# Six FFN blocks of 256 tokens behind the first, with new places for the attention stages, in a fused retention and bilinear FFN kernel

## The chip, the cores and the metric

The kernel runs on one core of a Trainium2 chip. The metric is device time in microseconds (us), the median of the runs in the fast state; lower is better. The engines are PE (matmul), PEld (its weight loads), DVE, ACT and POOL; SP issues most DMAs. PSUM is the memory in which the code places the results of its matmuls. Every execution has a state, slow when it is over 1.5% above the fastest of the same kernel.

## The reference, cut to what matters

```python
# q, k, v: (8, 8, 576, 64)   batch, heads, sequence, head dim
scores = scale * q @ k.T
ret    = scores * D            # D[i, j] = gamma_h ** (i - j) for i >= j, else 0
attn   = ret @ v               # -> x: 4608 tokens x 512
a, b   = x @ w_a, x @ w_b      # 512 -> 1536
out    = (a * b) @ w_out       # 1536 -> 512, float32
```

## The kernel before

The 4608 tokens are 36 chunks of 128. Attention of a chunk (with a running state in place of the full score matrix) writes 128 columns of `xT`; the FFN reads `xT` block by block. PE runs both from one stream (in the profile after, where an output waits for DVE until 186.61 us, the FFN group behind it starts after it, at 187.15 us): the FFN is a generator that yields after every matmul, and attention stages are dropped into it at fixed places. A place is counted in units, one unit being the work of one 512-column matmul.

```python
blocks = [512, 256, 384, 384] + [512] * ((NTOK - 1536) // 512)

def ffn_block(tok0, n, runs):
    # ... for each of 12 column tiles F of d_ff:
        pa = ps_ffn.tile(...)                    # ps_ffn: 3 PSUM buffers
        # 4 matmuls of n columns; then on ACT:
        nc.scalar.copy(ha[:, 0:n], pa[:, 0:n])
        pb = ps_ffn.tile(...)
        # 4 matmuls of n columns; then on DVE:
        nc.vector.tensor_tensor(hT[:, F, 0:n], has[F][:, 0:n], pb[:, 0:n], op=ALU.mult)
        pop()                                    # ONE deferred DVE piece (a mask or a scaling)
        yield n / 512, True                      # an edge: stages may start here
    # ... then n/128 output groups po, 12 matmuls each, two pop() in each
```

```python
def second_stage(g):            # g: a pair of chunks
    for i in g[1:]: state(i)
    for i in g: scores(i)       # PE; defers two masks per chunk: later.append(...)
def third_stage(g):
    flush()                     # issue all masks that are still deferred
    for i in g: outputs(i)      # PE reads the masked scores sT

# ... places (chunks, cast and turn, scores, outputs), in units:
placed = [((6, 7), 145, 178, 194), ((8,), 166, 197, 207), ((9, 10), 186, 224, 254)]
limit = 1e9
for i in range(NCH - 1, 10, -2):
    g = (i, i + 1) if i + 1 < NCH else (i,)
    third = min(starts[i] - 16, limit - 60)
    limit = third
    placed.append((g, third - 104, third - (30 if i == 11 else 36), third))
# ... at the end of every FFN block: flush()
```

From chunk 6 on, q and k are cast on POOL and turned by a DMA that SP issues ("turn"); SP also issues loads and stores.

Of the kernel before, what the change touches and what calls it, by code (L numbers as in the profile page):

```python
# [18 lines left out]
def kernel(  # L19
# [19 lines left out]
    nc = tc.nc  # L39
# [3 lines left out]
    DFF = moe_w_a.shape[1]  # L43
    NTOK = B * S
    NC = DM // 128
    NF = DFF // 128
# [4 lines left out]
    NCH = NTOK // 128  # L51
# [14 lines left out]
    def pool(name, bufs, space=None):  # L66
        kw = {} if space is None else {"space": space}
        return ctx.enter_context(tc.tile_pool(name=name, bufs=bufs, **kw))
# [5 lines left out]
    qkt_pool = pool("qkt", 6)  # L74
    st_pool = pool("st", 4)
    h_pool = pool("hT", 2)
    ha_pool = pool("ha", 6)
    o_pool = pool("osb", 4)
    PS = bass.MemoryType.PSUM
    ps_ffn = pool("ps_ffn", 3, PS)  # L80
# [5 lines left out]
    wa_r = moe_w_a.rearrange("(c p) f -> p c f", p=128)  # L86
    wb_r = moe_w_b.rearrange("(c p) f -> p c f", p=128)
    wo_r = moe_w_out.rearrange("(c p) m -> p c m", p=128)
    wa_sb = big.tile([128, NC, DFF], BF16)
    wb_sb = big.tile([128, NC, DFF], BF16)  # L90
# [69 lines left out]
        nc.vector.memset(t, 0.0)  # L160

    def load_w(f0, f1):
        nc.gpsimd.dma_start(wa_sb[:, :, f0:f1], wa_r[:, :, f0:f1])
        nc.gpsimd.dma_start(wb_sb[:, :, f0:f1], wb_r[:, :, f0:f1])

    def load_wo(i):
        nc.gpsimd.dma_start(wo_sb[:, 4 * i:4 * i + 4, :],
# [6 lines left out]
    def pop():  # L174
        if later:
            later.pop(0)()

    def flush():
        while later:
            later.pop(0)()  # L180

    def cast(i, on="pool"):

        qf, kf, vf = staged.pop(i)
        qkb = nat.tile([128, 2, DM], BF16, tag="qkb", name="qkb")
        vb = nat.tile([128, DM], BF16, tag="vb", name="vb")
        qb, kb = qkb[:, 0], qkb[:, 1]
        if on == "pool":
            nc.gpsimd.tensor_copy(qb, qf)  # L189
        else:  # L190
            nc.scalar.copy(qb, qf)  # L191
        if on == "dve":
            nc.vector.tensor_copy(kb, kf)
        else:
            nc.gpsimd.tensor_copy(kb, kf)  # L195
        nc.gpsimd.tensor_tensor(  # L196
            vb.rearrange("p (h d) -> p h d", h=H),
            vf.rearrange("p (h d) -> p h d", h=H),
            vs[:, i % PER, :].unsqueeze(2).to_broadcast([128, H, D]),
            op=ALU.mult)  # L200
        natural[i] = (qkb, qb, kb, vb)
# [9 lines left out]
    def transposes(i):  # L211

        natural_qk = natural[i][1:3]
        qkT = qkt_pool.tile([128, 2, HP, 128], BF16, tag="qkT", name="qkT")
        for w, copy in ((0, nc.scalar.copy), (1, nc.vector.tensor_copy)):
            tp = ps_att.tile([128, HP, 128], BF16, tag="att", name="tp")
            for p in range(HP):
                nc.tensor.transpose(tp[:, p, :],  # L218
                                    natural_qk[w][:, p * 128:(p + 1) * 128],
                                    identity)  # L220
            copy(qkT[:, w], tp)
        transposed[i] = qkT

    def state(i):
        m = i % PER
        if m == PER - 1:
            return
        qkb, qb, kb, vb = natural[i]
        r = slice(64, 128) if m == MID else slice(0, 128)
        if m == 0 or m == MID:  # L230
            kv_of[0] = ps_kv.tile([128, HP, 128], FP32, tag="kv", name="kv")
        kv = kv_of[0]
        for p in range(HP):
            sl = slice(p * 128, (p + 1) * 128)
            nc.tensor.matmul(kv[:, p, :], kb[r, sl], vb[r, sl],  # L235
                             start=(m in (0, MID) and p == 0), stop=True,
                             skip_group_check=True)
        st = states[i % len(states)]
        state_of[i + 1] = st
        nc.scalar.copy(st[0:64, :, 0:64], kv[0:64, :, 0:64])  # L240
        nc.scalar.copy(st[64:128, :, 64:128], kv[64:128, :, 64:128])

    def scores(i):
        qkT = transposed[i]
        ps = [ps_att.tile([128, HP, 128], FP32, tag="att", name=f"sc{hi}")
              for hi in (0, 1)]
        sT = st_pool.tile([128, 2, HP, 128], BF16, tag="sT", name="sT")
        scored[i] = sT
        for p in range(HP):
            for hi in (0, 1):  # L250
                r = slice(64 * hi, 64 * hi + 64)
                nc.tensor.matmul(ps[hi][:, p, :], qkT[r, 1, p, :],  # L252
                                 qkT[r, 0, p, :], start=True, stop=True,
                                 skip_group_check=True)
        keep = mask2 if i % PER == MID else mask

        def masked(hi):
            nc.vector.tensor_tensor(
                sT[:, hi], ps[hi],
                keep.unsqueeze(1).to_broadcast([128, HP, 128]),  # L260
                op=ALU.mult)

        later.append(lambda: masked(0))
        later.append(lambda: masked(1))

    def outputs(i, halves=False):
        m = i % PER
        qkb, qb, kb, vb = natural.pop(i)
        qkT = transposed.pop(i)
        sT = scored.pop(i)  # L270
        o = ps_att.tile([128, HP, 128], FP32, tag="att", name="o")
        if m > 0:
            st = state_of.pop(i)
            n = 64 if m == MID else 128
            for p in range(HP):
                for hi in (0, 1):
                    nc.tensor.matmul(o[64 * hi:64 * hi + 64, p, 0:n],  # L277
                                     st[:, p, 64 * hi:64 * hi + 64],
                                     qkT[:, 0, p, 0:n],
                                     start=(p == 0), stop=True,  # L280
                                     skip_group_check=True)
        for p in range(HP):
            for hi in (0, 1):
                e0 = p * 128 + 64 * hi
                nc.tensor.matmul(o[64 * hi:64 * hi + 64, p, :],  # L285
                                 vb[:, e0:e0 + 64], sT[:, hi, p, :],
                                 start=(m == 0 and p == 0), stop=True,
                                 skip_group_check=True)
        s0 = rows_of(i)[0][3]

        def scaled(c0, c1):
            nc.vector.tensor_tensor(  # L292
                xT[:, c0:c1, i * 128:(i + 1) * 128], o[:, c0:c1],
                qs[:, c0:c1, s0:s0 + 128], op=ALU.mult)

        if halves:
            later.append(lambda: scaled(0, HP // 2))
            later.append(lambda: scaled(HP // 2, HP))
        else:
            later.append(lambda: scaled(0, HP))  # L300


    blocks = [512, 256, 384, 384] + [512] * ((NTOK - 1536) // 512)
    WCOLS = [3, 4, 5]

    def ffn_block(tok0, n, runs):

# [60 lines left out]
    def warm(count):  # L368

        w = ps_ffn.tile([128, 4, 128], FP32, tag="ab", name="w")  # L370
        for _ in range(count):
            nc.tensor.matmul(w, identity,  # L372
                             identity.unsqueeze(1).to_broadcast([128, 4, 128]),
                             start=True, stop=True)

    W1, W2 = 128 * WCOLS[0], 128 * (WCOLS[0] + WCOLS[1])
    idle = {0: (0, 0), 1: (0, 3), 2: (2, 4), 3: (1, 4)}
    make_qs(0)
    make_qs(1)
# [4 lines left out]
    for i in range(4):  # L384
        if idle[i][0]:
            warm(idle[i][0])
        scores(i)
        flush()
        if i == 2:
            load_w(0, W1)  # L390
            load_w(W1, W2)
        if i < 3:
            cast(i + 1, "dve" if i == 2 else "act")
        state(i)
        if idle[i][1]:
            warm(idle[i][1])
        if i < 3:
            transposes(i + 1)
            outputs(i)
            flush()  # L400
    load_w(W2, DFF)
    for i in (0, 1, 2):
        load_wo(i)
    outputs(3, halves=True)
# [10 lines left out]
    starts, at = {}, 0.0  # L415
# [50 lines left out]
    for i, places in ((4, (110, 117, 121, 127)), (5, (127, 132, 136, 139))):  # L466
        todo += [(at, one_by_one, (what, i))
                 for at, what in zip(places, "CTSA")]
    placed = [((6, 7), 145, 178, 194), ((8,), 166, 197, 207),
              ((9, 10), 186, 224, 254)]  # L470
    limit = 1e9
    for i in range(NCH - 1, 10, -2):
        g = (i, i + 1) if i + 1 < NCH else (i,)
        third = min(starts[i] - 16, limit - 60)
        limit = third
        placed.append((g, third - 104, third - (30 if i == 11 else 36), third))
    for g, zeroth, second, third in placed:
        todo += [(zeroth, ahead, (g[-1],)), (second - 14, first_stage, (g,)),
                 (second, second_stage, (g,)), (third, third_stage, (g,))]
# [2 lines left out]
    at = 0.0  # L482
    tok = 0
    for tb, n in enumerate(blocks):
        runs = WCOLS if tb == 0 else [1] * NF
        for cost, edge in ffn_block(tok, n, runs):
            at += cost
            while todo and edge and at >= todo[0][0]:
                _, fn, args = todo.pop(0)
                fn(*args)  # L490
        flush()
        tok += n
# [30 lines left out]
```

## Time and profile before

| | before |
|---|---|
| time, median of 3 runs | 346.02 us (345.85 to 346.22) |
| span of the profiled execution | 877.8 us, state slow |

The page of that profile: the span, the busy time of each engine, and the DMA engines' busy tenths in 40 slices of the span.

```profile
span 877.8 us, 6134 instructions
...
PE 854.0 (97%) x2390; PEld 309.4 (35%) x2426; DVE 162.0 (18%) x272; ACT 112.6 (13%) x229; POOL 84.3 (10%) x121
...
DMA  9980049350090041025400650066002300000000
```

From its chain of waits in order of time (start, length, what):

```profile
318.47 2.35 PE pa L316 x4
320.81 2.48 PE pb L329 x4
323.30 2.35 PE pa L316 x4
```

Four 512-column matmuls take 2.35 us, 587 ns each. The profiled execution is 2.5 times as long as a timed one. (The mean clock of 1.00 given for this profile is no measurement: its trace holds no clock record.) An unchanged copy of the kernel, run later (before_again), left a profile in the fast state, and it is the one to compare with. Its page, same rows, with the granted clock in tenths:

```profile
span 344.6 us, 6170 instructions
...
PE 330.4 (96%) x2426; PEld 171.4 (50%) x2426; DVE 160.8 (47%) x272; ACT 112.3 (33%) x229; POOL 85.0 (25%) x121
...
PEclk9999999999999999999999999999999999999999
DMA  9999999999999993911994099507990950020002
```

PE is the bound (96% busy), and the DMA engines are at 9 tenths or more in each of the first 15 slices (129 us). The busy share of PE does not tell a slow execution from a fast one: it is 97% at 877.8 us and 96% at 344.6 us.

### The profile page before, as it was taken

Reading aid. Unit: us, or ns where it says so; the run is one execution under the profiler, and the core shown is the slowest. Engines: PE = TensorE matmul, PEld = TensorE weight load, DVE = VectorE, ACT = ScalarE, POOL = GpSimd, SP = SyncE. Lnnn points to the kernel's source line nnn. Section 1 sums busy time; section 2 is a strip of 40 time slices with the busy share of each in tenths; the row PEclk is TensorE's granted clock in tenths of the full one; section 3 lists DMA queues with packets and bytes.
Section 4 is the critical chain, followed back from the end, with each engine's and each line's share of the span. In section 5 each row is a group of like instructions: output and inputs, shape, how many; then the busy total and the mean of one; then the engine's idle time right before and its main releaser. Section 6 shows DMA issues by size and latency. Waiting matters only on the chain.

```text
span 877.8 us, 6134 instructions
## 1 busy us (share of the span) xinstructions
PE 854.0 (97%) x2390; PEld 309.4 (35%) x2426; DVE 162.0 (18%) x272; ACT 112.6 (13%) x229; POOL 84.3 (10%) x121
## 2 busy tenths in 40 slices
PE   6999999999999999999999999999999999999998
PEld 3322345344344333333333333432333333232223
DVE  4211122222121111211122112121121112201100
ACT  5111112011011101100111011101110011101110
POOL 6040002201011010002100210011000000000000
DMA  9980049350090041025400650066002300000000
GB/s 181 207 152 0 25 90 187 80 88 1 29 199 0 13 102 18 0 50 108 81 1 1 131 108 1 0 112 129 0 1 60 61 0 1 8 28 12 0 13 36
DMA packets 154333, 50.74 MB, mean 58 GB/s; under 512 B 144960, under 2 KB 149824, under 8 KB 154304
## 3 DMA queue, kind: packets, MB, share of 16 engines
q1 hardware_dynamic: 149552, 45.63, 26.6%
q0 software_dynamic: 4752, 4.72, 3.4%
q8 instruction: 19, 0.31, 0.2%
q14 instruction: 10, 0.08, 0.0%
HBM read 37.75 MB, written 9.44 MB: 54 GB/s over the span
## 4 chain that ended last, share of the span: by engine, by line
PE 97%; issue 2%; DMA 1%; SPq 0%; POOL 0%; DVE 0%; ACT 0%
PE pb L329 29%; PE pa L316 29%; PE po L349 28%; PE o L285 2%; PE kv L235 2%; PE o L277 2%; PE w L372 1%; PE tp L218 1%; DMA kf<-in_k_dram 1%; SPq L104 0%; POOL qkb L195 0%; PE sc_2460 L252 0%; PE sc_2449 L252 0%; PE sc_1402 L252 0%; PE sc_3677 L252 0%
## 5 line engine op out<-in xcount | busy, mean ns | idle before, releaser
L329 PE MATMUL pb<-xT,wb_sb 128*128 128x512 bf16 (+2 forms) x471 | 279.9, 775 | 2.7 <-issue 2.7
L316 PE MATMUL pa<-xT,wa_sb 128*128 128x512 bf16 (+2 forms) x472 | 277.3, 769 | 3.6 <-issue 3.1
L349 PE MATMUL po<-wo_sb,hT 128*128 128x512 bf16 (+1 forms) x425 | 253.2, 810 | 6.2 <-issue 6.2
L334 DVE TENSOR_TENSOR hT<-ha,pb 128x512 bf16<-128x512 bf16 (+2 forms) x120 | 76.2, 635 | 457.4 <-PE pb L329 443.3
L329 PEld LDWEIGHTS <-wb_sb 128*128 128x128 bf16 x480 | 82.8, 172 | 173.7 <-issue 168.0
L316 PEld LDWEIGHTS <-wa_sb 128*128 128x128 bf16 x480 | 80.7, 172 | 157.2 <-issue 151.4
L349 PEld LDWEIGHTS <-hT 128*128 128x128 bf16 x444 | 73.1, 169 | 162.1 <-issue 159.0
L322 ACT CAST ha<-pa 128x512 bf16<-128x512 f32 (+2 forms) x120 | 65.2, 544 | 447.1 <-PE pa L316 440.9
L196 POOL TENSOR_TENSOR vb<-vf,vs 128x512 bf16<-128x512 f32 x36 | 37.6, 1044 | 295.1 <-issue 144.3
L189 POOL CAST qkb<-qf 128x512 bf16<-128x512 f32 x30 | 18.3, 611 | 290.5 <-DMA qf<-in_q_dram 274.6
L360 DVE COPY osb<-po 128x512 f32<-128x512 f32 (+1 forms) x17 | 11.5, 676 | 175.5 <-PE po L349 175.5
L358 ACT COPY osb<-po 128x512 f32<-128x512 f32 (+1 forms) x20 | 11.5, 576 | 219.3 <-PE po L349 208.4
L292 DVE TENSOR_TENSOR xT<-o,qs 128x512 bf16<-128x512 f32 (+1 forms) x37 | 24.8, 674 | 46.8 <-PE o L285 46.8
L285 PE MATMUL o<-sT,vb 128*64 128x128 bf16 x288 | 30.4, 379 | 0.0
L235 PE MATMUL kv<-vb,qkb 128*128 128x128 bf16 (+1 forms) x128 | 25.4, 373 | 1.4 <-issue 0.9
L235 PEld LDWEIGHTS <-qkb 128*128 128x128 bf16 (+1 forms) x128 | 17.6, 161 | 22.2 <-issue 20.9
L285 PEld LDWEIGHTS <-vb 128*64 128x64 bf16 x288 | 22.3, 181 | 2.5 <-issue 2.5
L195 POOL CAST qkb<-kf 128x512 bf16<-128x512 f32 x32 | 19.7, 616 | 13.6 <-DMA kf<-in_k_dram 13.5
L252 PEld LDWEIGHTS <-qkT 64*128 64x128 bf16 x288 | 15.4, 135 | 12.6 <-issue 9.8
L218 PE MATMUL tp<-identity,qkb 128*128 128x128 bf16 x48 | 8.1, 362 | 6.0 <-ACT qkb L191 5.3
L372 PE MATMUL w<-identity 128*128 128x512 bf16 x14 | 9.3, 790 | 0.0
L218 PEld LDWEIGHTS <-qkb 128*128 128x128 bf16 x48 | 5.2, 140 | 11.1 <-ACT qkb L191 5.7
(195 smaller groups left out, 194.7 us busy)
## 6 DMA issues: line engine op xcount, KB each, us to landing
out_dram<-osb SPq DMA_DIRECT2D x35, 256.0 KB, 2.2
qf<-in_q_dram SPq DMA_DIRECT2D x32, 256.0 KB, 3.6
kf<-in_k_dram SPq DMA_DIRECT2D x32, 256.0 KB, 4.2
vf<-in_v_dram SPq DMA_DIRECT2D x32, 256.0 KB, 4.7
wo_sb<-in_moe_w_out_dram POOLq DMA_DIRECT2D x3, 512.0 KB, 17.8
qf<-in_q_dram SPq DMA_DIRECT2D x8, 128.0 KB, 3.6
kf<-in_k_dram SPq DMA_DIRECT2D x8, 128.0 KB, 3.5
vf<-in_v_dram SPq DMA_DIRECT2D x8, 128.0 KB, 3.5
```

The costliest lines, as they stand in the source:

```text
L189: nc.gpsimd.tensor_copy(qb, qf)
L195: nc.gpsimd.tensor_copy(kb, kf)
L196: nc.gpsimd.tensor_tensor(vb.rearrange("p (h d) -> p h d", h=H), vf.rearrange("p (h d) -> p h d", h=H), vs[:, i % PER, :].unsqueeze(2).to_ ...
L218: nc.tensor.transpose(tp[:, p, :], natural_qk[w][:, p * 128:(p + 1) * 128], identity)
L235: nc.tensor.matmul(kv[:, p, :], kb[r, sl], vb[r, sl], start=(m in (0, MID) and p == 0), stop=True, skip_group_check=True)
L285: nc.tensor.matmul(o[64 * hi:64 * hi + 64, p, :], vb[:, e0:e0 + 64], sT[:, hi, p, :], start=(m == 0 and p == 0), stop=True, skip_group_che ...
L292: nc.vector.tensor_tensor(xT[:, c0:c1, i * 128:(i + 1) * 128], o[:, c0:c1], qs[:, c0:c1, s0:s0 + 128], op=ALU.mult)
L316: nc.tensor.matmul(pa[:, 0:n], wa_sb[:, c, fs], xT[:, c, tok0:tok0 + n], start=(c == 0), stop=(c == NC - 1))
L322: nc.scalar.copy(ha[:, 0:n], pa[:, 0:n])
L329: nc.tensor.matmul(pb[:, 0:n], wb_sb[:, c, fs], xT[:, c, tok0:tok0 + n], start=(c == 0), stop=(c == NC - 1))
L334: nc.vector.tensor_tensor(hT[:, F, 0:n], has[F][:, 0:n], pb[:, 0:n], op=ALU.mult)
L349: nc.tensor.matmul(po[:, 0:width], hT[:, F, u * 128:(u + 1) * 128], wo_sb[:, F, cols], start=(F == 0), stop=(F == NF - 1))
```

## The change

Its intent: every block from the second to the seventh takes 256 tokens, so that each has exactly one pair of chunks to wait for, and all later pairs line up with even chunks. At start-up, k of chunk 3 is cast on DVE between the two masks of chunk 2, and one weight DMA is issued later.

```diff
-    blocks = [512, 256, 384, 384] + [512] * ((NTOK - 1536) // 512)
+    blocks = [512] + [256] * 6 + [512] * ((NTOK - 2048) // 512)
@@ start-up, chunk i of the first four
         scores(i)
-        flush()
-        if i == 2:
-            load_w(0, W1)
-            load_w(W1, W2)
-        if i < 3:
-            cast(i + 1, "dve" if i == 2 else "act")
+        pop()                          # first mask only
+        if i == 2:
+            list(load_w(0, W1))        # load_w is now a generator of two DMAs
+            second = load_w(W1, W2)
+            next(second)               # its other DMA after the loop
+        if i == 2:
+            cast(3, "dve")
+            flush()
+        else: ...
@@ places
-    placed = [((6, 7), 145, 178, 194), ((8,), 166, 197, 207),
-              ((9, 10), 186, 224, 254)]
+    placed = [((6, 7), 145, 176, 200), ((8, 9), 186, 238, 264),
+              ((10, 11), 222, 296, 324), ((12, 13), 280, 352, 384)]
-    for i in range(NCH - 1, 10, -2):
-        third = min(starts[i] - 16, limit - 60)
-        placed.append((g, third - 104, third - (30 if i == 11 else 36), third))
+    for i in range(NCH - 2, 13, -2):
+        third = min(starts[i] - 16, limit - 58)
+        placed.append(((i, i + 1), third - 104, third - 36, third))
```

Cut: `ha_pool` from 6 to 7 buffers, a renamed list, and the generator itself.

More of the change, by code (lines that the diff above doesn't have):

```diff
@@ L76 @@
     h_pool = pool("hT", 2)
-    ha_pool = pool("ha", 6)
+    ha_pool = pool("ha", 7)
     o_pool = pool("osb", 4)
@@ L162, in load_w @@
     def load_w(f0, f1):
-        nc.gpsimd.dma_start(wa_sb[:, :, f0:f1], wa_r[:, :, f0:f1])
-        nc.gpsimd.dma_start(wb_sb[:, :, f0:f1], wb_r[:, :, f0:f1])
+        for w_sb, w_r in ((wa_sb, wa_r), (wb_sb, wb_r)):
+            nc.gpsimd.dma_start(w_sb[:, :, f0:f1], w_r[:, :, f0:f1])
+            yield
     def load_wo(i):
@@ L300, in outputs @@
             later.append(lambda: scaled(0, HP))
-    blocks = [512, 256, 384, 384] + [512] * ((NTOK - 1536) // 512)
-    WCOLS = [3, 4, 5]
+    blocks = [512] + [256] * 6 + [512] * ((NTOK - 2048) // 512)
+    WRUNS = [3, 4, 5]
     def ffn_block(tok0, n, runs):
@@ L374, in warm @@
                              start=True, stop=True)
-    W1, W2 = 128 * WCOLS[0], 128 * (WCOLS[0] + WCOLS[1])
+    W1, W2 = 128 * WRUNS[0], 128 * (WRUNS[0] + WRUNS[1])
     idle = {0: (0, 0), 1: (0, 3), 2: (2, 4), 3: (1, 4)}
@@ L387 @@
         scores(i)
-        flush()
+        pop()
         if i == 2:
-            load_w(0, W1)
-            load_w(W1, W2)
-        if i < 3:
-            cast(i + 1, "dve" if i == 2 else "act")
+            list(load_w(0, W1))
[4 more added lines that the diff above has]
+            flush()
+        else:
+            flush()
+            if i < 3:
+                cast(i + 1, "act")
         state(i)
@@ L400 @@
             flush()
-    load_w(W2, DFF)
+    list(second)
+    list(load_w(W2, DFF))
     for i in (0, 1, 2):
@@ L468 @@
                  for at, what in zip(places, "CTSA")]
-    placed = [((6, 7), 145, 178, 194), ((8,), 166, 197, 207),
-              ((9, 10), 186, 224, 254)]
+    placed = [((6, 7), 145, 176, 200), ((8, 9), 186, 238, 264),
+              ((10, 11), 222, 296, 324), ((12, 13), 280, 352, 384)]
     limit = 1e9
-    for i in range(NCH - 1, 10, -2):
-        g = (i, i + 1) if i + 1 < NCH else (i,)
-        third = min(starts[i] - 16, limit - 60)
+    for i in range(NCH - 2, 13, -2):
+        third = min(starts[i] - 16, limit - 58)
         limit = third
-        placed.append((g, third - 104, third - (30 if i == 11 else 36), third))
+        placed.append(((i, i + 1), third - 104, third - 36, third))
     for g, zeroth, second, third in placed:
@@ L484 @@
     for tb, n in enumerate(blocks):
-        runs = WCOLS if tb == 0 else [1] * NF
+        runs = WRUNS if tb == 0 else [1] * NF
         for cost, edge in ffn_block(tok, n, runs):
```

## The prediction

> **The profile is not the timed state.** The timed runs take 346.0 us; the profiled execution spans 877.8 us and is marked slow. In the timeline four 128x512 matmuls take 2.35 us (587 ns each) and eight 128x256 ones 2.34 to 2.48 us.[...] Other engines' durations I take from the trace.
>
> **What bounds it.** PE: 97% busy, 97% of the chain of waits. The FFN is 1296 matmuls of 512 columns' worth[...]. Scores run in pairs (two start 10 ns apart in the timeline); the attention of 32 chunks behind the FFN is then 16 slots of 128 columns[...]. The first FFN matmul starts at 29.6 us in the trace[...].[...]
>
> **What the change moves.**
> 1. Start-up: k of chunk 3 is cast (0.42 us) before the second mask (0.68 us) on DVE, so its transposes can start about 0.6 us earlier. In the trace the four filler matmuls (2.6 us at 587 ns) hide this[...]. Estimate -0.4 us. The last wb piece, issued a microsecond later, has slack.
> 2. Blocks: 256, 384, 384 and two 256s of a 512 become six 256s.[...]
> 3. Evacuation:[...] DVE needs 0.42 for hT, and 1.1 when one mask (0.68) or xT scaling (0.69) is popped behind it[...]. The old 256 block carries six masks and three scalings[...]; the new six carry four and two each[...].
> 4. Feeding: the chain of cast, turn, load on POOL and SP gives a chunk every 4.6 us in the trace (loads 126.2, 130.6, 135.0, 140.0), turns land 4.0 us after issue. Before, chunks 6 to 8 are wanted inside one block of 72 units[...] and 9 to 12 soon after, within a few units of when their turns land; after, each pair has a block of its own. This should remove 1.5 to 3 us of PE waits at scores, which the slow profile cannot show.
>
> Sum about -1: **345.0 us**, range **342.0 to 347.8**. Faster by over 2%: 0.03; within 2%: 0.94; slower by over 2%: 0.03.
>
> **What would show it.** A profile in the fast state: DVE releasing PE at pa or pb in 256-token blocks (3), no wait of scores on a turn (4). If it is slow again, only times tell (undoing the blocks alone, or the cast order alone); its span should be within 1% of before, with 576 pa and pb weight loads each against 480.
>
> **What would make it wrong.** Feed stalls larger than I think (gain 3 to 5 us); DVE contention stronger than the PSUM slack (loss 2 to 4)[...].

Terms are cut from it, because they rested on matmul times that the one trace it had did not show: its budget of the whole time, which came to 340 to 349 us, the reason why point 1 should count in a fast run although fillers hide it in the trace, and the terms of points 2 and 3, +0.5 and +1.3 us. With -0.4 (point 1) and -1.5 to -3 (point 4) the sum came to "about -1", as it says.

## More of the kernel before

A stage can start only at an *edge*, which comes after each `pb` group (every 8 units in a 512-token block, every 4 in a 256-token one) and at some points of the output stage.

Who made PE wait in the fast execution (total us, times, longest; the `tp` line is start-up, where PE waits for its first data):

```profile
PE tp L218 <- ACT qkb L191: 5.7, 2, 5.3
PE sc L252 <- DMA qkT<-qkb: 2.4, 3, 1.3
...
PE o L285 <- DVE sT L258: 0.2, 1, 0.2
```

The idle time in this view is counted from a modelled end of the matmul before. What a wait costs is larger and is read from start to start: two `sc` matmuls that follow each other in 0.06 us otherwise stand 1.51 us apart at 79.7 us. Measured so, the waits between 56 and 94 us cost 0.53 + 0.35 + 1.46 + 0.90 = 3.2 us (chunks 7, 7, 10 and 12). The 0.35 us is a wait of `outputs` for a mask; the other three, 2.9 us, are waits of scores for a turned tile:

```profile
65.61 0.40 PE L252 MATMUL sc<-qkT 64*128 64x128 bf16 x8 [0.37 <-DMA qkT<-qkb]
...
81.21 0.40 PE L252 MATMUL sc<-qkT 64*128 64x128 bf16 x8 [1.30 <-DMA qkT<-qkb]
...
93.22 0.42 PE L252 MATMUL sc<-qkT 64*128 64x128 bf16 x8 [0.73 <-DMA qkT<-qkb]
```

## The result, and the profile after

| | median | range | runs |
|---|---|---|---|
| before | 345.94 us | 345.74 to 346.22 | 4 |
| after | 349.65 us | 349.40 to 351.13 | 4 |

The ratio is 1.0116 (95% interval 1.0086 to 1.0145). A ratio here is the mean time of one kernel's fast runs over that of the other's of the same rounds, so not quite the ratio of the medians. The change is 3.7 us slower: within 2%, but outside the predicted range. This profile came in the fast state. Its page, the same rows, the clock again included:

```profile
span 347.7 us, 6608 instructions
...
PE 329.7 (95%) x2584; PEld 190.4 (55%) x2618; DVE 163.2 (47%) x297; ACT 115.5 (33%) x252; POOL 84.7 (24%) x121
...
PEclk9999999999999999999999999999999999999999
DMA  9999999999899989868490299519980990020002
```

PE's waits:

```profile
PE tp L219 <- ACT qkb L192: 5.8, 2, 5.3
PE o L286 <- DVE sT L259: 2.4, 4, 0.6
PE sc L253 <- DMA qkT<-qkb: 1.7, 2, 0.9
...
PE pb L330 <- ACT ha L323: 0.5, 1, 0.5
```

The wait for turned tiles has shrunk from 2.4 us to 1.7 us, in two places:

```profile
64.32 0.40 PE L253 MATMUL sc<-qkT 64*128 64x128 bf16 x8 [0.94 <-DMA qkT<-qkb]
65.50 0.40 PE L253 MATMUL sc<-qkT 64*128 64x128 bf16 x8 [0.79 <-DMA qkT<-qkb]
```

In the list of waits a new line stands above it: `outputs` waits four times for a mask (`sT`). Where in time does the loss lie? The start of the first `ha` cast of each block marks PE's progress:

| token where the block starts | before_again | after | after minus before |
|---|---|---|---|
| 0 | 22.44 | 21.77 | -0.67 |
| 512 | 56.91 | 56.25 | -0.66 |
| 2048 | 170.47 | 169.41 | -1.06 |
| 2560 | 205.90 | 205.88 | -0.02 |
| 3072 | 240.99 | 241.78 | +0.79 |
| 3584 | 276.64 | 278.04 | +1.40 |
| 4096 | 311.05 | 314.17 | +3.12 |
| end | 344.57 | 347.69 | +3.12 |

At token 2048, where the 256-token blocks end, the kernel after is *ahead* by 1.06 us. All of the loss arises behind them, in blocks of 512 tokens that look the same in both kernels. (One chunk's attention, about 0.9 us, has moved over this border: by the places in the code the kernel before has finished 21 chunks at token 2048, the kernel after 20. So up to token 2048 the two kernels are about even, the earlier start included, and the stretch behind it loses 4.18 - 0.9 = 3.3 us. The two traced runs, 346.27 and 349.40 us, differ by 3.1 us, the medians by 3.7.)

Here is one of those blocks in the kernel after. PE first, in order of time (start, length, what, and in brackets the idle time before it and what ended it):

```profile
177.53 0.62 PE L253 MATMUL sc<-qkT 64*128 64x128 bf16 x16
...
184.13 1.03 PE L330 MATMUL pb<-xT,wb_sb 128*128 128x512 bf16 x4
185.09 0.41 PE L278 MATMUL o<-qkT,state 128*64 128x128 bf16 x8
...
185.78 0.22 PE L286 MATMUL o<-sT,vb 128*64 128x128 bf16 x1
186.61 0.38 PE L286 MATMUL o<-sT,vb 128*64 128x128 bf16 x7 [0.60 <-DVE sT L259]
```

DVE in the same stretch:

```profile
184.15 0.68 DVE L259 TENSOR_TENSOR sT<-sc,mask 128x512 bf16<-128x512 f32 x1
185.27 0.69 DVE L335 TENSOR_TENSOR hT<-ha,pb 128x512 bf16<-128x512 bf16 x1 [0.44 <-PE pb L330]
185.87 0.68 DVE L259 TENSOR_TENSOR sT<-sc,mask 128x512 bf16<-128x512 f32 x1
```

The last mask starts at 185.87 us, behind the `hT` multiply of the last `pb` group; the output matmul that reads it would have started at 185.83 and starts at 186.61, 0.77 us late before rounding. The other three blocks show the same 0.77 us at 222, 258 and 294 us. (The whole stretch of output matmuls takes 1.93 us there, against 1.11 us without the wait in after_60, so a wait costs up to 0.82 us.) The same stretch of before_again:

```profile
176.83 0.64 PE L252 MATMUL sc<-qkT 64*128 64x128 bf16 x13
...
186.14 0.41 PE L277 MATMUL o<-qkT,state 128*64 128x128 bf16 x8
...
186.74 0.39 PE L285 MATMUL o<-sT,vb 128*64 128x128 bf16 x8
```

No wait: 9.3 us lie between scores and outputs, where the kernel after has 7.6 us. The difference is one step of 8 units. The places explain it. In the block that starts at unit 576, the spacing of 60 gave outputs at 644 and scores at 608, which is exactly on the edge 32 units into the block. The spacing of 58 gives 646 and 610: the outputs still start at the same edge (72 units in), but the scores miss the edge at 32 and start at 40. One mask is popped at each `pb` group, so five groups between the two give four masks and one group to spare; four groups put the fourth mask directly before the matmul that needs it. The other blocks repeat it: 790, 934 and 1078 are all 70 units into their blocks.

### The profile page after: what moved, and what is told of

Same layout as the page of the kernel before. It is cut to its first block, busy times and chain, and to the rows that moved or that the text cites. A ratio compares the mean times of both kernels' runs of the same rounds, so it can differ in the third digit from the quotient of the medians.

```text
span 347.7 us, 6608 instructions
## 1 busy us (share of the span) xinstructions
PE 329.7 (95%) x2584; PEld 190.4 (55%) x2618; DVE 163.2 (47%) x297; ACT 115.5 (33%) x252; POOL 84.7 (24%) x121
## 4 chain that ended last, share of the span: by engine, by line
PE 89%; SPq 3%; DMA 3%; DVE 2%; issue 1%; POOL 1%; ACT 0%; DVEq 0%
PE pa L317 27%; PE pb L330 26%; PE po L350 26%; SPq L104 3%; PE sc L253 2%; PE o L286 2%; PE kv L236 2%; PE o L278 2%; DMA vf<-in_v_dram 1%; DMA qkT<-qkb 1%; DVE hT L335 1%; DVE sT L259 1%; POOL vb L197 1%; DMA out_dram<-osb 1%; PE tp L219 0%
## 5 line engine op out<-in xcount | busy, mean ns | idle before, releaser
L335 DVE TENSOR_TENSOR hT<-ha,pb 128x512 bf16<-128x512 bf16 (+1 forms) x144 | 79.6, 553 | 104.7 <-PE pb L330 95.9
L317 PE MATMUL pa<-xT,wa_sb 128*128 128x512 bf16 (+1 forms) x569 | 114.9, 325 | 1.1 <-DVE xT L293 0.5
L330 PE MATMUL pb<-xT,wb_sb 128*128 128x256 bf16 (+1 forms) x567 | 114.7, 325 | 0.9 <-ACT ha L323 0.5
L323 ACT CAST ha<-pa 128x512 bf16<-128x512 f32 (+1 forms) x144 | 69.0, 479 | 138.0 <-PE pa L317 131.5
L350 PE MATMUL po<-wo_sb,hT 128*128 128x512 bf16 (+1 forms) x426 | 96.4, 373 | 1.3 <-issue 0.5
L330 PEld LDWEIGHTS <-wb_sb 128*128 128x128 bf16 x576 | 56.3, 98 | 38.2 <-issue 0.6
L317 PEld LDWEIGHTS <-wa_sb 128*128 128x128 bf16 x576 | 54.4, 98 | 38.0 <-issue 1.3
L350 PEld LDWEIGHTS <-hT 128*128 128x128 bf16 x444 | 41.9, 98 | 45.8
L259 DVE TENSOR_TENSOR sT<-sc,mask 128x512 bf16<-128x512 f32 x72 | 47.7, 683 | 6.0 <-PE sc L253 4.5
L286 PE MATMUL o<-sT,vb 128*64 128x128 bf16 x288 | 14.9, 222 | 2.4 <-DVE sT L259 2.4
```

The source lines that it names most:

```text
L259: nc.vector.tensor_tensor(sT[:, hi], ps[hi], keep.unsqueeze(1).to_broadcast([128, HP, 128]), op=ALU.mult)
L286: nc.tensor.matmul(o[64 * hi:64 * hi + 64, p, :], vb[:, e0:e0 + 64], sT[:, hi, p, :], start=(m == 0 and p == 0), stop=True, skip_group_che ...
L317: nc.tensor.matmul(pa[:, 0:n], wa_sb[:, c, fs], xT[:, c, tok0:tok0 + n], start=(c == 0), stop=(c == NC - 1))
L330: nc.tensor.matmul(pb[:, 0:n], wb_sb[:, c, fs], xT[:, c, tok0:tok0 + n], start=(c == 0), stop=(c == NC - 1))
L350: nc.tensor.matmul(po[:, 0:width], hT[:, F, u * 128:(u + 1) * 128], wo_sb[:, F, cols], start=(F == 0), stop=(F == NF - 1))
```

## The experiments

Theory A: the loss is this fourth mask of a pair, four times 0.77 us. Theory B, the rival and the fear of the prediction: DVE contention and small matmuls in the 256-token blocks.

### 1. Which part of the change

No edit (before_again), the start-up alone on the kernel before (startup_only), and the kernel after with the old start-up (blocks_only).

> The kernel before, unchanged, for a profile in the fast state. Every theory: 345.7 to 346.3 us, ratio 1.000. If the profile is fast: the feed theory of the prediction expects PE waits at scores for turned tiles of 1.5 to 3 us more than the 1.7 us that the kernel after shows; its rival (the feed before was as good or better) expects no more than 1.7 us.

> The kernel before with only the start-up part of the change (k of chunk 3 cast between the masks, the last wb piece of the second run issued later). Prediction: -0.4 us, 345.5 us. Rival, that the later wb piece or the later second mask costs more: slower, up to 347.

> The kernel after with the start-up of before. If the loss of 3.7 us lies all in the 256-token blocks and their places: 349.6 to 350.1 us, about 0.4 above the kernel after. If the start-up part is to blame: near 346.

before_again: 346.18 us, ratio 1.0004 (0.9989 to 1.0019). startup_only: 346.43 us, 1.0014 (0.9996 to 1.0032). blocks_only: 349.53 us, 1.0101 (1.0085 to 1.0118). The loss is in the blocks and places. (The waits for turned tiles, 2.4 us against 1.7, fall between the two expectations of before_again: the feed of the kernel before was worse, but by 0.7 us in this view and not by 1.5 to 3. The expected -0.4 us of startup_only did not show.) The start-up gains nothing on its own, although its FFN starts 0.47 us earlier (20.91 against 21.38 us). PE's timeline of startup_only shows where that went:

```profile
64.76 0.40 PE L253 MATMUL sc<-qkT 64*128 64x128 bf16 x8 [0.42 <-DMA qkT<-qkb]
65.73 0.40 PE L253 MATMUL sc<-qkT 64*128 64x128 bf16 x8 [0.57 <-DMA qkT<-qkb]
...
72.95 0.40 PE L253 MATMUL sc<-qkT 64*128 64x128 bf16 x8 [0.85 <-DMA qkT<-qkb]
```

The second of these scores starts at 65.73, in before_again at 65.61: that turned tile arrives when it arrives, and an earlier PE waits longer for it. The third line, chunk 8, is something else: its tile landed at 72.90 us, in before_again at 71.50, so the arrivals themselves differ between executions. This trace is of the slowest of the four runs (347.36 us).

### 2. The spacing: taken back in two ways, and put into the kernel before

```diff
# after_60
-        third = min(starts[i] - 16, limit - 58)
+        third = min(starts[i] - 16, limit - 60)
# after_38 (spacing 58 kept)
-        placed.append(((i, i + 1), third - 104, third - 36, third))
+        placed.append(((i, i + 1), third - 104, third - 38, third))
# before_58 (all else as before)
-        third = min(starts[i] - 16, limit - 60)
+        third = min(starts[i] - 16, limit - (58 if i > 20 else 60))
```

> The kernel after with the spacing of pairs set back from 58 to 60 units. Theory A (the loss is the fourth mask of a pair, issued one step before the outputs that read it, in four of the 512-token blocks, 0.77 us each): those four waits vanish, -3.1 us, 346.5 us, ratio 1.000 to 1.003. Theory B (the loss is the 256-token blocks themselves, DVE and small matmuls): no change, 349.5 us, ratio 1.010.

> The kernel after with the spacing of 58 kept, and the scores two units earlier instead (third minus 38 in place of minus 36), which brings them one step earlier in the four blocks and leaves the outputs where they are. Theory A: same gain, 346.5 us. Theory B, or if the place of the outputs matters rather than the distance: 349.5 us.

> The kernel before with the spacing set to 58 for chunks from 21 on alone, all blocks as before. Theory A: four waits of 0.77 us appear in its 512-token blocks, +3.1 us, 349.1 us, ratio 1.009. Theory B: 346.0 us, ratio 1.000.

| | median | ratio to before | 95% interval |
|---|---|---|---|
| after_60 | 346.72 | 1.0013 | 0.9986 to 1.0040 |
| after_38 | 347.56 | 1.0018 | 0.9979 to 1.0056 |
| before_58 | 350.06 | 1.0101 | 1.0085 to 1.0116 |

Before, in the same rounds, took 346.61 us. Theory A holds all three times, theory B in none. Putting the one number into the kernel before, with none of the small blocks, costs as much as the whole change, and its trace has the wait in the same place:

```profile
187.12 0.22 PE L285 MATMUL o<-sT,vb 128*64 128x128 bf16 x1
188.04 0.38 PE L285 MATMUL o<-sT,vb 128*64 128x128 bf16 x7 [0.70 <-DVE sT L258]
```

In the traces of after_60 and after_38 the four waits are gone. In these four blocks all three edits come to the same thing: they move the scores between the edges 32 and 40, and the outputs stay at the edge 72 (places 644 and 646 are both rounded up to it). That the distance in edges counts, and not the edge of the scores as such, is read from the DVE lines above; no run moved the outputs alone.

after_38 has two kinds of run: 346.16 and 346.48, but 348.63 and 349.53 us. The profiled runs of after_60 (348.07) and after_38 (349.53) are of the second kind. PE's timeline of after_60:

```profile
65.12 0.40 PE L253 MATMUL sc<-qkT 64*128 64x128 bf16 x8 [1.49 <-DMA qkT<-qkb]
65.96 0.40 PE L253 MATMUL sc<-qkT 64*128 64x128 bf16 x8 [0.44 <-DMA qkT<-qkb]
66.29 1.03 PE L317 MATMUL pa<-xT,wa_sb 128*128 128x256 bf16 x4
```

and its windows (stretch, length, busy times, then granted clock, DMA share, which this view can put above 1, and GB/s):

```profile
56.00:66.00 10.00, 8.07 (x83) 6.83 (x82) 4.06 (x9) 4.45 (x12) 3.75 (x5) 1.00 1.04 238
66.00:70.00 4.00, 4.00 (x27) 2.87 (x28) 1.07 (x3) 0.74 (x2) 1.23 (x2) 0.57 1.23 210
```

When the tiles of chunks 6 and 7 come late, the two waits cost 1.65 + 0.60 us within 2.6 us, and in the 4 us behind them the granted clock is 0.57 on average: 4 x 0.43 = another 1.7 us, an estimate. (Four 256-column matmuls take 0.83 us there, from 66.29 to 67.12 us, against 0.43 us at 62.38.) after_38, after 2.24 + 1.01 us, has 0.81 between 66 and 70 us and 0.91 between 70 and 80. The profiled run of the kernel after lost 1.11 + 0.95 us there and kept its clock (1.00 in all three windows); its slowest run, 351.13 us, has a mean clock of 0.995 as these two have, but left no trace that could say where.

### 3. Turns ahead of the stores in SP's queue

```diff
# before_early
-    placed = [((6, 7), 145, 178, 194), ...
+    placed = [((6, 7), 134, 178, 194), ...
# before_actout
-                nc.sync.dma_start(out[rows, cols], osb[:, cols])
+                (nc.scalar if tok0 == 0 else nc.sync).dma_start(out[rows, cols], osb[:, cols])
```

> The kernel before with the casts and turns of chunks 6 and 7 placed at 134 units instead of 145, so that they stand ahead of the four stores of the first block in the SP queue. Feed theory (PE waits of 0.5, 0.3, 1.5 and 0.9 us at scores and outputs of chunks 7 to 10 come from the turns standing behind those stores, about 2.8 us late): 1.5 to 3 us of waits go, 343 to 344.5 us. Rival (the transfers are bound by the DMA engines[...], so the order in the queue does not matter): 346 us, ratio 1.000.

> The kernel before with the four stores of its first block issued by the ACT queue in place of the SP queue (before_early moved only one of them behind the turns, 0.6 us, and settled nothing). If the turns of 6 and 7 are late because they stand behind those stores: they issue at about 57.6 in place of 60.3 us, the waits at chunks 7 to 10 shrink by 1.5 to 3 us, 343.5 to 344.5 us. If the DMA engines themselves are the limit: 346 us.

before_early: 346.33 us, 0.9995 (0.9979 to 1.0011). This was a miss in its design: only one of the four stores came to stand behind the turns (SP issues them at 59.68 us in place of 60.25), so it tested little. The two turns landed 0.7 and 0.5 us earlier and the wait at chunk 7 was gone, but the tile of chunk 8 landed 0.4 us later, and PE now lost 0.47 us there. before_actout: 348.41 us, 1.0050 (1.0036 to 1.0064), slower. The turn of chunk 6 did issue at 57.53 us, that of chunk 7 only at 61.23 (61.89 in before_again), and PE's wait for turned tiles left the list of waits. But ACT's own work now stood behind the stores: PE lost 1.3, 0.9 and 1.2 us around 47 to 55 us, and the second block started 3.9 us late (60.84 against 56.91 us), which alone gives the turns more time. And the turn of chunk 6, issued 2.7 us earlier, landed only 0.4 us earlier (64.29 against 64.67 us). So its place in SP's queue was not what set its landing in this run; whether the busy DMA engines did was not tested and stays open.

### 4. Filling the waits that are left

```diff
# a60_67: after_60, with
-    placed = [((6, 7), 145, 176, 200), ...
+    placed = [((6, 7), 145, 184, 204), ...
+    todo.append((208, flush, ()))
# a60_both: a60_67, with
-              ... ((12, 13), 280, 352, 384)]
+              ... ((12, 13), 280, 364, 388)]
# a60_both_oldstart: a60_both with the start-up of before
```

> after_60 with the scores of chunks 6 and 7 two steps later (184 in place of 176 units), their outputs at 204 and the scalings flushed at 208. If the 1.3 to 3.2 us that PE waits there for the turned tiles is time that FFN work can fill: -1 to -1.7 us against after_60, 345.2 us. If that work is only moved and the wait turns up at the next pair: no change, 346.7 us.

> a60_67 with the scores of chunks 12 and 13 at 364 in place of 352 units (388 for the outputs), so that their masks are not flushed three at once at the end of a 256-token block. If that burst is what makes PE wait 0.62 us for ha and 0.19 for pb's buffer: -0.8 us against a60_67, 344.4 us, ratio to before 0.994 to 0.996. Otherwise as a60_67.

> a60_both with the start-up of before. If the start-up's 0.6 us is real and was only given back at the wait for chunks 6 and 7, it shows now that this wait is filled: +0.4 to +0.6 us against a60_both. If it never counted: equal within 0.2 us.

In the same rounds before took 346.63 us. a60_67: 344.86 us, 0.9948 (0.9934 to 0.9961). a60_both: 343.60 us, 0.9916 (0.9903 to 0.9930). a60_both_oldstart: 344.08 us, 0.9938 (0.9916 to 0.9961). The wait for chunks 6 and 7 is time that FFN work can fill: start to start it is 0.77 us in the trace of a60_67, 2.25 in that of after_60. In a60_67 a 0.62 us gap still stands at 113.8 us before a `pb` group, as in the kernel after, where DVE does three masks in a row:

```profile
113.28 1.88 DVE L259 TENSOR_TENSOR sT<-sc,mask 128x512 bf16<-128x512 f32 x3
115.07 0.74 DVE L335 TENSOR_TENSOR hT<-ha,pb 128x256 bf16<-128x256 bf16 x2
```

(DVE of the kernel after.) The `pb` group that waits, in the same trace:

```profile
115.52 0.60 PE L330 MATMUL pb<-xT,wb_sb 128*128 128x256 bf16 x4 [0.46 <-ACT ha L323]
```

The scores at 352 left one edge before the block's end at 360, where `flush()` issues the other three masks together. In a60_both, with the scores at 364, that gap is gone, and with it one of the three waits of 0.19 us before a `pa` group that a60_67 has. The gain on a60_67 is 1.3 us in medians, more than the 0.8 expected; the rest is not explained. Only 1.0 us of waiting for a turn is left behind the start-up (1.2 us from start to start), all of it in one place:

```profile
PE sc L253 <- DMA qkT<-qkb: 1.0, 1, 1.0
...
PE pa L317 <- DVE xT L293: 0.5, 1, 0.5
```

### 5. What was still open: the start-up, and the blocks themselves

before_retimed keeps the old blocks, takes the new start-up, and moves back the stages whose waits were long.

```diff
-              ((9, 10), 186, 224, 254)]
+              ((9, 10), 186, 234, 264)]
+        late = 10 if i == 11 else 0     # chunks 11 and 12
-        placed.append((g, third - 104, third - (30 if i == 11 else 36), third))
+        placed.append((g, third - 104,
+                       third + late - (30 if i == 11 else 36), third + late))
```

> The blocks of before with the new start-up, and the stages of chunks 9 and 10 (scores 234, outputs 264 in place of 224 and 254) and of 11 and 12 (ten units later) moved back, so that the waits of 1.5 and 0.9 us there are filled. If the gain of a60_both comes from where stages stand and not from the 256-token blocks: 343.3 to 344.3 us, as a60_both. If the small blocks are needed for it: 345.5 us or more.

> a60_both once more on the same chip as the other two: 343.4 to 344.0 us, ratio 0.991 to 0.993.

> a60_both with the old start-up, with more rounds than the first time. If the start-up gives 0.4 us once the wait after it is filled: 343.9 to 344.5 us, 0.3 to 0.6 above a60_both_again. If it is worth nothing: within 0.2 us of it.

| | median | ratio to before (346.32 us) | 95% interval |
|---|---|---|---|
| before_retimed | 345.44 | 0.9970 | 0.9954 to 0.9986 |
| a60_both_again | 343.89 | 0.9927 | 0.9916 to 0.9939 |
| a60_both_oldstart_ag | 344.68 | 0.9952 | 0.9934 to 0.9970 |

Start-up: taking it back costs 0.9938 / 0.9916 = 1.0022 in one set of rounds and 0.9952 / 0.9927 = 1.0025 in the other, 0.8 to 0.9 us, or 0.5 and 0.8 us between the medians. The sign agrees in both sets, but the intervals overlap in both, and the first set leans on one execution, the traced one of 345.86 us, in which the FFN starts at 23.50 us; without it the means differ by 0.1 us. Of the seven fast traces with the old start-up two start that late (23.37 and 23.50 us, the others 21.38 to 21.70), of the eight with the new one none (20.71 to 21.49). So the size of the gain, and how much of it is such late starts, stays open. In the trace of startup_only it is given back at the waits for chunks 6 to 8.

Blocks: with old blocks the retiming took the wait at chunk 10 from 1.46 to 0.17 us, but chunks 6 and 7 now cost 0.50 + 1.21 us and chunk 12 still 0.87 us. The version with small blocks is 0.4% faster, and 345.44 us lies 0.06 us short of what was expected if the small blocks are needed. But this is one placement of the old blocks, not the best one, so neither that the small blocks are easier to feed nor that the old ones could not be placed as well is shown.

a60_both beats both kernels: 343.6 and 343.9 us in two sets of rounds, 3.0 and 2.4 us under before.

## Why the prediction was wrong

It said 345.0 us, between 342.0 and 347.8; it was 349.65. Point by point:

1. **Start-up, -0.4 us.** The FFN starts 0.67 us earlier in the kernel after (0.47 in startup_only): the mechanism held. That it would shorten the whole by itself was not borne out (startup_only, 1.0014): the lead is lost at the next waits for turned tiles. With those waits filled it is worth something between 0.1 and 0.9 us. Its other estimate, a start at 27 us in a fast run, was far off (21.4). The last `wb` piece did have slack: in the kernel after it is issued at 18.28 us, lands 8.8 us later and is first read at 29.13 us.
2. **Matmuls, +0.5 us** (the author's estimate, now cut). Right. 256-column matmuls follow each other every 109.1 ns, 512-column ones every 215.9, 384-column ones every 162.5 (means over pairs that nothing delays; the first two in the kernel after, the third in before_again). The 576 small ones of the kernel after cost 576 x 109.1 - 288 x 215.9 = 0.7 us more than full ones, the mixed ones of before 96 x 109.1 + 192 x 162.5 - 192 x 215.9 = 0.2 us. Weight loads did not show in the kernel after: those for `pa` and `pb` took 98 ns each on average, and with one before every matmul the 256-column ones still kept to 109.1 ns.
3. **DVE contention, +1.3 us net** (its two parts, 3 and 1.7 us). The net was about right, +1.0, but by luck: both of its parts were too large. The kernel after loses four times 0.19 us before a `pa` group and 0.62 us once, 1.4 us in sum (3 were predicted); before has none of these, only one 0.35 us wait for a mask (1.7 were predicted). That the 0.62 us is a burst of three masks, and not the steady load, was not foreseen.
4. **Feeding, -1.5 to -3 us.** The direction was right, the size was not: 0.53 + 1.46 + 0.90 = 2.9 us of waits of scores for turned tiles before, 1.11 + 0.95 = 2.1 us after, so 0.8 us were removed. "No wait of scores on a turn" did not come true: a block of its own did not bring the tiles of chunks 6 and 7 in time.
5. **The step that failed is the sum itself.** "Sum about -1" holds only these four terms, all of them before token 2048. Up to there the kernel after is 1.06 us ahead, of which about 0.9 is the moved chunk: about even, and the four terms as measured (-0.67 + 0.5 + 1.0 - 0.8) say the same. So the -1 was not there either; after_60, the change without the new spacing, takes 346.72 us against 346.61. Of the 4.65 us between 345.0 and 349.65 this missing 1 us is the smaller part. For the larger, the prediction took the 512-token blocks behind as unchanged and never asked what the new spacing, 58 for 60, does to them. It moves the scores of four pairs over an edge and leaves their outputs, and costs 4 x 0.77 = 3.1 us, a term that the sum does not have. "DVE contention stronger than the PSUM slack (loss 2 to 4)" named the right loser for the wrong reason: not a PSUM buffer of the FFN held too long, but a mask issued one step too late.

The chance of 0.94 for "within 2%" was right, but it was a statement about how little room there was.

## What to carry to other kernels

When stages are placed by numbers that are rounded up to the next allowed point, compute for every stage, also in the blocks that a change does not name, which point it lands on; a shift of two units cost 3 us, spread over four blocks that the change does not name. Where deferred work is issued one piece at each point, count the points between producer and consumer and keep one to spare, and let no block end with several pieces deferred. An earlier start can be lost at the next wait for data with its own arrival time, as here: fill that wait first, then count the gain.

## What the traces leave open

- What slowed the profile of the kernel before. Its 512-column matmuls follow each other mostly every 621 ns or every 485 ns, all through the 877.8 us; its weight loads for `pa` and `pb` take 172 ns on average, against 98 ns in the kernel after. The trace has no clock record, so whether this is another clock stays open.
- When the clock falls. Two waits of 1.65 and 0.60 us were followed by a granted clock of 0.57 over 4 us (after_60), and 2.24 and 1.01 us by 0.81 over 4 us and 0.91 over the 10 us after that (after_38); 1.11 and 0.95 us (the kernel after) were followed by 1.00. What tells these apart is not shown, nor that the waits are the cause.
- What sets the time at which a turn lands. Between 50 and 100 us it lands 3.7 to 6.4 us after its issue, median 4.7, in before_again, and 3.2 to 6.0 us, median 4.8, in the kernel after. In the first nine slices of the page of the kernel after (78 us) the DMA engines are at 9 tenths or more and move 173 to 252 GB/s. No run changed this load alone.
